# Windowed attention ahead of a SiLU MLP: attention in blocks with all heads, both key blocks side by side

## The chip, the cores and the metric

The kernel runs on one core of a Trainium2 chip. The metric is the device time of one execution in microseconds (us), the median of several runs. The engines are named as the profile names them: PE (TensorE, matrix products; PEld is its loading of weights), DVE (VectorE), ACT (ScalarE), POOL (GpSimd) and SP (SyncE, which issues most transfers).

## The reference

For 8 batches, 8 heads, 576 positions and head size 64 it computes attention in a causal window of 128 positions with a linear bias for each head, and sends the result (4608 tokens of 512 values) through an MLP with SiLU. Everything is float32; the MLP's weights are drawn as float64.

```python
scores = scale * np.matmul(q, k.transpose(0, 1, 3, 2))
mask = (rel >= 0) & (rel < window)
scores = np.where(mask, scores + bias[None], -1000000000.0)
attn = np.exp(scores - np.max(scores, axis=-1, keepdims=True))
attn = attn / (np.sum(attn, axis=-1, keepdims=True) + 1e-09)
x = np.matmul(attn, v)          # then to (tokens, 512)
h = x @ w_in                    # 512 x 2048
out = (h * (1.0 / (1.0 + np.exp(-h)))) @ w_out
```

## The kernel before, in words

**MLP.** Tokens go in nine groups of 512 (`TG`). For each group and each of 16 slices of the hidden size (`NF`) there are two half steps of the first product (`gemm1`, L464) and two of the second (`gemm2`, L499), of six products of 128x128 by 512 each. Every factor is split into a high and a low part of type float32r, and three of the four products of parts are made, so a group has 16 x 24 = 384 products. Between them stands the activation: tanh on ACT (`act1`, L471), a join on DVE (`act2`, L476), the high part on ACT (`act3`, L482), the low part `gl` (`act4`, L487) on POOL for the first 16 slices and on DVE for the others. In group 0 the weights are also converted: `w_next` loads float64 words, scales them on ACT (`w_split1`), joins three pieces on DVE (`w_shift` L533, `w_low` L538, `w_sign` L545), and takes the high part on ACT (L555) and the low part on POOL (L559); three of the 32 parts are converted ahead of the MLP.

**Attention.** Two batches follow each other in nine blocks of 128 rows (4 x 9 blocks in all). A unit is one block and two heads; there are 144 units and 16 ghosts, which only bring the keys and values of a block again. Inside a batch pair the order is heads first, blocks second (`plan`). A row of a block sees keys of its own block up to itself and of the block before behind itself, so exactly 128 keys; the kernel merges both blocks of scores into one tile of 128 columns: `soft1` (L277) copies the block before from PSUM on ACT, `soft_merge` (L286) lays the own block over it under a triangular mask on DVE. `row_max` (L292) adds the bias from `tab` and takes the row's maximum, `soft2` (L300) is the exponential on ACT. P is split into two float16 parts (`p_split`, L307 and L311), transposed by the DMA engines (L316), and parted again into its two key blocks by two selects on POOL (`p_select`, L355 and L358). `attend` (L382) multiplies with V, which is itself scaled by a power of two for each batch pair and split in two float16 parts (`v_hi` L222, `v_lo` L229). `normalize` divides by the sum and writes x, in two float16 parts from the ninth tile on.

The scores of the first 44 units (`QF`) come from float32 products of all 128 rows, with zeros in the other head's rows (L246). Later units split q and k in high and low parts (`qk_hi` on POOL L202 and L205, `q_lo` L210 and `k_lo` L215 on DVE) and make two float32r products of 256 columns for a head (L252). The first 16 units have P transposed by PE (L323) and V in float32.

**Order.** Each engine takes its instructions in the order in which the program writes them, and waits on semaphores that the framework sets. Ahead of the MLP `attn_cycle` runs 21 cycles of attention alone. From then on the points between half steps of the MLP are counted: `attn_item` puts a third of a cycle (scores; transposes; products with V) at a point, and `later(n, ...)` puts work of other engines n points later. PSUM has eight banks: tags `h` and `a` with two each, and `w`, `x`, `y`, `z`. During the MLP `w` to `z` hold the second product's sums, `h` the first's, and everything of attention shares `a`.

The scale of V needs a reduction over all V of a batch pair, nine reads and sums (`vscale_load`, `vscale_reduce`, `vscale_finish`).

## Time and profile before

| | |
|---|---|
| three runs | 1028.01 us median, 1027.22 to 1028.36 |
| span of the profiled execution, from its first to its last instruction | 1025.5 us; of its own time the profile gives no more than this |
| first product of the MLP | 52.7 us |
| first scaling of an output (group 0) | 211.5 us |
| busy: PE, DVE, ACT, POOL | 975.5, 748.8, 445.2, 450.6 us |
| mean granted clock of PE | 0.991 |
| transfers | 111.0 MB, of it HBM read 76.8 MB and written 9.4 MB |

Busy times are sums over the whole span; a share of it means little for a single stage, so the stages have to be looked at one by one. Products on PE are pipelined: the duration of one reaches into the next, and the pace is seen from the distances between starts. L12 is line 12 of the kernel.

### The profile page before, as it was taken

Reading aid. Unit: us, or ns where it says so; the run is one execution under the profiler, and the core shown is the slowest. Engines: PE = TensorE matmul, PEld = TensorE weight load, DVE = VectorE, ACT = ScalarE, POOL = GpSimd, SP = SyncE. Lnnn points to the kernel's source line nnn. Section 1 sums busy time; section 2 is a strip of 40 time slices with the busy share of each in tenths; the row PEclk is TensorE's granted clock in tenths of the full one; section 3 lists DMA queues with packets and bytes.
Section 4 is the critical chain, followed back from the end, with each engine's and each line's share of the span. In section 5 each row is a group of like instructions: output and inputs, shape, how many; then the busy total and the mean of one; then the engine's idle time right before and its main releaser. Section 6 shows DMA issues by size and latency. Waiting matters only on the chain.

```text
span 1025.5 us, 18152 instructions
## 1 busy us (share of the span) xinstructions
PE 975.5 (95%) x5832; PEld 798.2 (78%) x5832; DVE 748.8 (73%) x2306; ACT 445.2 (43%) x1039; POOL 450.6 (44%) x770
## 2 busy tenths in 40 slices
PE   7878777799999999999999999999999999999998
PEld 6866555678888888888888887888888888888886
DVE  4899999977777999777778997777699963223222
ACT  5755545444445444444444444343444442223222
POOL 2566576735344565543436665443465640001000
PEclk9999999899999999999999999999999999999999
DMA  8656565543345444543355445433453321011001
GB/s 288 198 145 193 178 176 162 157 113 104 83 106 131 119 109 122 131 115 88 91 115 130 121 116 140 96 81 74 119 119 98 98 81 27 1 21 42 1 1 41
DMA packets 166511, 111.04 MB, mean 108 GB/s; under 512 B 107920, under 2 KB 136592, under 8 KB 166416
## 3 DMA queue, kind: packets, MB, share of 16 engines
q1 hardware_dynamic: 165120, 107.53, 39.8%
q10 hardware_dynamic: 1296, 2.36, 0.7%
q8 instruction: 46, 0.75, 0.3%
q14 instruction: 49, 0.40, 0.1%
HBM read 76.81 MB, written 9.44 MB: 84 GB/s over the span
## 4 chain that ended last, share of the span: by engine, by line
PE 75%; DVE 16%; issue 4%; DMA 2%; ACT 2%; POOL 0%; SPq 0%; ACTq 0%; DVEq 0%; POOLq 0%
PE o L499 33%; PE h L464 32%; PE sp L252 4%; PE av L382 4%; DVE wm L538 3%; DVE v L229 2%; DVE wm L533 2%; DMA vm<-v 2%; DVE t L292 1%; DVE hr L311 1%; DVE t L286 1%; DVE wm L545 1%; PE sp L246 1%; DVE gt L476 1%; DMA rqk<-qk 1%
## 5 line engine op out<-in xcount | busy, mean ns | idle before, releaser
L464 PE MATMUL h<-xh,wih 128*128 128x512 f32 x576 | 231.7, 402 | 2.4 <-ACT wih L555 2.4
L499 PE MATMUL o<-woh,gh 128*128 128x512 f32 x576 | 231.6, 402 | 0.0
L464 PE MATMUL h<-xh,wil 128*128 128x512 f32 x576 | 227.5, 395 | 4.2 <-POOL wil L559 4.2
L499 PE MATMUL o<-woh,gl 128*128 128x512 f32 x576 | 227.8, 395 | 0.4 <-DVE gl L487 0.3
L499 PE MATMUL o<-wol,gh 128*128 128x512 f32 x576 | 226.9, 394 | 0.0
L464 PE MATMUL h<-xl,wih 128*128 128x512 f32 x576 | 226.4, 393 | 0.0
L476 DVE SCALAR_TENSOR_TENSOR gt<-gt,h 128x512 f32<-128x512 f32 x144 | 98.7, 685 | 141.8 <-ACT gt L471 141.2
L471 ACT ACTIVATE gt<-h 128x512 f32<-128x512 f32 x144 | 85.6, 594 | 199.3 <-PE h L464 197.8
L300 ACT ACTIVATE t<-t,mx 128x128 f32<-128x128 f32 x288 | 102.6, 397 | 146.7 <-DVE mx L292 143.2
L355 POOL TENSOR_SCALAR_AFFINE_SELECT po<-hl 128x512 f16<-128x512 f16 (+1 forms) x128 | 89.2, 697 | 116.5 <-DMA hl<-hr 98.8
L202 POOL TENSOR_SCALAR kh<-rqk 128x256 fp32r<-128x256 f32 x116 | 54.0, 465 | 182.4 <-PE sp L252 111.0
L464 PEld LDWEIGHTS h<-xh,wil 128*128 128x128 f32 x576 | 108.8, 189 | 31.5 <-POOL wil L559 7.6
L487 DVE TENSOR_TENSOR gl<-gt,gh 128x512 fp32r<-128x512 f32 x128 | 95.8, 749 | 49.5 <-ACT gh L482 48.6
L499 PEld LDWEIGHTS o<-woh,gl 128*128 128x128 f32 x576 | 108.3, 188 | 27.8 <-DVE gl L487 2.4
L464 PEld LDWEIGHTS h<-xh,wih 128*128 128x128 f32 x576 | 109.4, 190 | 23.5 <-ACT wih L555 3.5
L464 PEld LDWEIGHTS h<-xl,wih 128*128 128x128 f32 x576 | 109.3, 190 | 20.3 <-DVE xl L434 0.2
L499 PEld LDWEIGHTS o<-wol,gh 128*128 128x128 f32 x576 | 108.5, 188 | 20.4
L499 PEld LDWEIGHTS o<-woh,gh 128*128 128x128 f32 x576 | 108.4, 188 | 20.1
L482 ACT CAST gh<-gt 128x512 fp32r<-128x512 f32 x144 | 89.3, 620 | 52.9 <-DVE gt L476 50.6
L292 DVE CUSTOM_DVE_ANT_0 t<-t,tab 128x128 f32<-128x128 f32 x288 | 99.8, 383 | 4.8 <-DMA tab<-base 0.7
L358 POOL TENSOR_SCALAR_AFFINE_SELECT hl<-hl 128x512 f16<-128x512 f16 (+1 forms) x128 | 95.6, 747 | 8.8
L277 ACT COPY t<-sp 128x256 f32<-128x256 f32 (+2 forms) x128 | 45.3, 354 | 94.0 <-PE sp L252 79.6
(81 smaller groups left out, 1481.9 us busy)
## 6 DMA issues: line engine op xcount, KB each, us to landing
rqk<-qk SPq DMA_DIRECT2D x144, 256.0 KB, 2.8
rv<-v SPq DMA_DIRECT2D x144, 64.0 KB, 2.1
out<-ot SPq DMA_DIRECT2D x36, 256.0 KB, 2.0
wr<-w_in SPq DMA_DIRECT2D x16, 512.0 KB, 3.9
wr<-w_out SPq DMA_DIRECT2D x16, 512.0 KB, 3.5
vm<-v SPq DMA_DIRECT2D x27, 256.0 KB, 3.0
vm<-v ACTq DMA_DIRECT2D x9, 256.0 KB, 5.0
rqk<-qk SPq DMA_DIRECT2D x16, 128.0 KB, 2.2
```

The costliest lines, as they stand in the source:

```text
L202: nc.gpsimd.tensor_scalar(kh[:, s], rqk[:, 1], 1.0, 1.0, op0=ALU.mult, op1=ALU.mult)
L277: nc.scalar.copy(t[rows, :, cols], sp[rows, :, o, cols])
L292: nc.vector.tensor_tensor_reduce(out=t[:, h], in0=t[:, h], in1=tab[:, 2 * hp + h], scale=-0.125, scalar=3.0e38, op0=ALU.add, op1=ALU.min, ...
L300: nc.scalar.activation(t[:, h], t[:, h], AF.Exp, bias=mx[:, h : h + 1], scale=-1.0)
L355: nc.gpsimd.affine_select(out=po, in_=hl, pattern=dims + [[-1, P]], base=-1, channel_multiplier=1, compare_op=ALU.is_ge, fill=0.0)
L358: nc.gpsimd.affine_select(out=hl, in_=hl, pattern=dims + [[1, P]], base=0, channel_multiplier=-1, compare_op=ALU.is_ge, fill=0.0)
L464: nc.tensor.matmul(hps[n], w[:, cc], x, start=(half == 0 and i == 0), stop=(half == 1 and i == len(seq) - 1), skip_group_check=True,)
L471: nc.scalar.activation(gt, hps[n], AF.Tanh, scale=0.5 / W_SCALE)
L476: nc.vector.scalar_tensor_tensor(out=gt, in0=gt, scalar=1.0, in1=hps[n], op0=ALU.add, op1=ALU.mult)
L482: nc.scalar.copy(gh, gt)
L487: (nc.gpsimd if GLP(n) else nc.vector).tensor_sub(gl, gt, f32(gh))
L499: nc.tensor.matmul(ops[ti], a[:, t], w, start=(f == 0 and i == 0), stop=(f == NF - 1 and i == len(seq) - 1), skip_group_check=True,)
```

## The change

Attention is written anew. The unit of work is now a pair: one block and four heads (`p`, two to a block, 72 in all). Blocks come in order, each with all heads, so there are no ghosts; keys and queries of a block are loaded once for all heads (256 KB each, against 256 KB for each unit before).

- **Scores** are float32 products for every block. The tile has the 64 rows of one head in its upper half and those of the next in its lower half; each product takes 64 rows, and neighbouring products are of different halves and go to different PSUM banks. The splitting of q and k is gone.
- **Both key blocks lie side by side** in tiles of 256 columns. `tab` holds the bias for 256 columns with -1e30 where the window ends, so the copy, the merge and the two selects are gone; the maxima read PSUM directly, and the exponentials, both parts of P and its transposes are twice as wide. Where two batches meet, DVE writes the mask into PSUM (`other_batch`).
- **P** is always transposed by the DMA engines, and V always in two float16 parts, a whole block of 512 columns at a time.
- **x** of the first four tiles is float32 and is transposed by PE; later ones are multiplied to float32 and split on ACT and DVE (`x_hi`, `x_lo`).
- **Engines**: `gl` is made on POOL in all groups; the low parts of `w_in` are made on DVE, those of `w_out` still on POOL. Four weight parts are converted ahead of the MLP.
- **Order**: one list of points. Pair p has its scores at point 8(p - 8) - 26 and its other work at fixed distances from there; points below 0 lie ahead of the MLP, and a group of the MLP has 64 points. During the MLP the scores of a pair take both buffers of tag `a`, which products with V and the scales of V use too.

```diff
-NPAIR = H // 2
+NHP = H // 2
...
+NPAIR = 2 * NTILE
...
-KSLOTS = 4
-VSLOTS = 5
+KSLOTS = 3
+VSLOTS = 3
...
+STEP = 8
+LEAD = 26
+XD = GT
...
+WD = (1, 1, 1, 2, 3)
+W_EARLY = (-52, -40, -28, -14)
...
+def at(p):
+    return STEP * (p - 2 * GT) - LEAD
...
-    tab = const.tile([P, H, P], BF16, name="tab")
+    tab = const.tile([P, H, 2 * P], BF16, name="tab")
...
-    bank = {"scores": ["a"], "pt": ["a"], "av": ["a"], "misc": ["a"]}
+    bank = {"scores": [("w", "x"), ("y", "z")], "av": ["a"], "misc": ["h"]}
...
-        tag = (LAST[-1], LAST[-2], "vraw")[i % 3 if b == 0 else 2]
+        tag, bufs = (LAST[4 + i % 4], 1) if b == 0 else ("rv", 2)
...
-    def qk_hi(u):
...
-    def q_lo(u):
...
-    def k_lo(u):
...
-    def soft0(u):
...
-    def soft1(u):
...
-    def soft_merge(u):
...
-    def p_select(u):
...
+    def load_k(i):
+        ks[i] = pool.tile([P, NHP, P], F32, tag="k", bufs=KSLOTS, name=f"k{i}")
+        nc.sync.dma_start(ks[i], qk[i, 1])
+    def load_q(i):
+        qs[i] = pool.tile([P, NHP, P], F32, tag="q", bufs=2, name=f"q{i}")
+        nc.sync.dma_start(qs[i], qk[i, 0])
+    def v_hi(i):
+        rv = rvs[i].rearrange("p (h d) -> p h d", h=H)
+        nc.gpsimd.tensor_scalar(
+            v1[:, i % VSLOTS, :, 0:D], rv, vsc[i // NBLK][:, 0:1], 1.0, op0=ALU.mult, op1=ALU.mult
+        )
+    def v_lo(i):
+        rv = rvs.pop(i).rearrange("p (h d) -> p h d", h=H)
+        nc.vector.scalar_tensor_tensor(
+            out=v2[:, i % VSLOTS], in0=rv, scalar=vsc[i // NBLK][:, 0:1], in1=v1[:, i % VSLOTS, :, 0:D],
+            op0=ALU.mult, op1=ALU.subtract,
+        )
+    def scores(p):
+        i, q = divmod(p, 2)
+        tags = next_tag("scores")
+        sp = [ps_of(tags[h], f"sp{p}_{h}").rearrange("p (u o c) -> p u o c", u=2, o=2) for h in range(2)]
+        for u in range(2):
+            for o in range(blocks(p).start, 2):
+                for h in range(2):
+                    rows = slice(h * D, (h + 1) * D)
+                    nc.tensor.matmul(
+                        sp[h][:, u, o], qs[i][rows, 2 * q + u], ks[i - 1 + o][rows, 2 * q + u],
+                        start=True, stop=True, skip_group_check=True,
+                    )
+        st[p] = {"sp": sp, "t": {}, "hl": {}, "mx": pool.tile([P, 4], F32, tag="mx", bufs=4, name=f"mx{p}")}
+    def other_batch(p):
+        for h in range(2):
+            cols = st[p]["sp"][h].rearrange("p u o c -> p u (o c)")
+            if block_of(p // 2) == SPLIT:
+                nc.vector.memset(cols[HALF:, :, : P + HALF], MASKED)
+            elif block_of(p // 2) == SPLIT + 1:
+                nc.vector.memset(cols[:, :, :HALF], MASKED)
+    def row_max(p, u):
+        q, o = p % 2, blocks(p)
+        n = (o.stop - o.start) * P
+        st[p]["t"][u] = t = pool.tile([P, 2, 2 * P], F32, tag="t", bufs=3, name=f"t{p}_{u}")
+        for h in range(2):
+            nc.vector.tensor_tensor_reduce(
+                out=t[:, h, 2 * P - n :], in0=st[p]["sp"][h][:, u, o].rearrange("p o c -> p (o c)"),
+                in1=tab[:, 4 * q + 2 * u + h, 2 * P - n :], scale=-0.125, scalar=3.0e38,
+                op0=ALU.add, op1=ALU.min, accum_out=st[p]["mx"][:, 2 * u + h : 2 * u + h + 1],
+            )
+    def exps(p, u):
+        t, n = st[p]["t"][u], (2 - blocks(p).start) * P
+        for h in range(2):
+            x = t[:, h, 2 * P - n :]
+            nc.scalar.activation(x, x, AF.Exp, bias=st[p]["mx"][:, 2 * u + h : 2 * u + h + 1], scale=-1.0)
+    def split_of(p, u, what):
+        n = 2 - blocks(p).start
+        return what[:, : 4 * n * P].rearrange("p (a h c) -> p a h c", a=2, h=2)
+    def p_hi(p, u):
+        t, n = st[p]["t"][u], (2 - blocks(p).start) * P
+        st[p]["hr", u] = hr = pool.tile([P, 8 * P], F16, tag="hr", bufs=2, name=f"hr{p}_{u}")
+        nc.scalar.activation(split_of(p, u, hr)[:, 0], t[:, :, 2 * P - n :], AF.Copy, scale=PSCALE)
+    def p_lo(p, u):
+        t, n = st[p]["t"][u], (2 - blocks(p).start) * P
+        hr = split_of(p, u, st[p]["hr", u])
+        nc.vector.scalar_tensor_tensor(
+            out=hr[:, 1], in0=t[:, :, 2 * P - n :], scalar=PSCALE, in1=hr[:, 0], op0=ALU.mult, op1=ALU.subtract
+        )
+    def p_transpose(p, u):
+        n = 2 - blocks(p).start
+        hr = st[p].pop(("hr", u))
+        st[p]["hl"][u] = hl = pool.tile([P, 8, P], F16, tag="hl", bufs=4, name=f"hl{p}_{u}")
+        nc.sync.dma_start_transpose(hl[:, : 4 * n], hr[:, : 4 * n * P])
...
+    def normalize(p, stage):
+        (i, q), av = divmod(p, 2), st[p]["av"]
+        if stage == 0:
+            st[p]["r"] = r = pool.tile([P, 4, 1], F32, tag="r", bufs=3, name=f"r{p}")
+            total = av[:, :, D : D + 1]
+            if i < XD:
+                nc.vector.tensor_scalar(r, total, PSCALE * EPS, vsc[i // NBLK][:, 0:1], op0=ALU.add, op1=ALU.mult)
+            else:
+                nc.vector.tensor_scalar_add(r, total, PSCALE * EPS)
+            nc.vector.reciprocal(r, r)
+            return
+        if i < XD:
+            if i not in xt:
+                xt[i] = pool.tile([P, DM], F32, tag=LAST[i], bufs=1, name=f"x{i}")
+            x = xt[i][:, q * 4 * D : (q + 1) * 4 * D]
+        else:
+            st[p]["x"] = x = pool.tile([P, 4 * D], F32, tag="xs", bufs=2, name=f"xs{p}")
+        nc.vector.tensor_mul(
+            x.rearrange("p (h d) -> p h d", h=4), av[:, :, 0:D], st[p]["r"].to_broadcast([P, 4, D])
+        )
+    def x_hi(p):
+        i, q = divmod(p, 2)
+        if i < XD:
+            return
+        if q == 0:
+            xt[i] = pool.tile([P, 2, DM], F16, tag="x", bufs=4, name=f"x{i}")
+        nc.scalar.copy(xt[i][:, 0, q * 4 * D : (q + 1) * 4 * D], st[p]["x"])
+    def x_lo(p):
+        i, q = divmod(p, 2)
+        if i >= XD:
+            cols = slice(q * 4 * D, (q + 1) * 4 * D)
+            nc.vector.tensor_sub(xt[i][:, 1, cols], st[p]["x"], xt[i][:, 0, cols])
+            if q == 1:
+                whole.append(i)
+        del st[p]
...
-        (nc.gpsimd if GLP(n) else nc.vector).tensor_sub(gl, gt, f32(gh))
+        nc.gpsimd.tensor_sub(gl, gt, f32(gh))
...
-        nc.gpsimd.tensor_sub(lo, wraw.pop((f, which))[1], f32(hi))
+        (nc.gpsimd if which else nc.vector).tensor_sub(lo, wraw.pop((f, which))[1], f32(hi))
...
+    for p in range(NPAIR):
+        i, q = divmod(p, 2)
+        n = at(p)
+        put(n, scores, p)
+        if block_of(i) in (SPLIT, SPLIT + 1):
+            put(n + 1, other_batch, p)
+        put(n + 1, row_max, p, 0)
+        put(n + 2, row_max, p, 1)
+        put(n + 2, exps, p, 0)
+        put(n + 3, exps, p, 1)
+        put(n + 3, p_hi, p, 0)
+        put(n + 4, p_lo, p, 0)
+        put(n + 4, p_hi, p, 1)
+        put(n + 4, p_transpose, p, 0)
+        put(n + 5, p_lo, p, 1)
+        put(n + 5, p_transpose, p, 1)
+        put(n + 20, attend, p)
+        put(n + 21, normalize, p, 0)
+        put(n + 22, normalize, p, 1)
+        put(n + 23, x_hi, p)
+        put(n + 24, x_lo, p)
+        if q == 0:
+            if i > 1:
+                put(n - 14, load_q, i)
+                put(n - 14, load_k, i)
+            put(n - 2, load_v, i)
+            put(n + 9, v_hi, i)
+            put(n + 10, v_lo, i)
+    for b in range(1, NBB):
+        n = at(2 * NBLK * b)
+        for i in range(VCH):
+            put(n - 10 * STEP + i * STEP, vscale_load, b, i)
+            put(n - 10 * STEP + i * STEP + 6, vscale_reduce, b, i)
+        for x in range(3):
+            put(n - 6 + 2 * x, vscale_finish, b, x)
...
+        while pos[0] < 0:
+            begin()
+            pos[0] += 1
+        bank.update(scores=[("a", "a")], misc=["a"])
...
+                        later(1, act2, n)
+                        later(2, act3, n)
+                        later(2, act4, n)
...
+                if g == 0 and half == 0:
+                    w_next()
```

More of the change, by code (lines that the diff above doesn't have):

```diff
@@ L279, in soft_merge @@
-    def soft_merge(u):
-        b, hp, j, _ = units[u]
-        sp, d, o = st[u]["sp"]
-        t = st[u]["t"]
-        for a in (slice(0, HALF), slice(HALF, P)) if j == SPLIT else (slice(0, P),):
-            n = a.stop - a.start
-            mask = tri.bitcast(I32)[a, :, a].to_broadcast([n, 2, n])
-            nc.vector.copy_predicated(t[a, :, a], mask, sp[a, :, d, a])
-    def row_max(u):
-        b, hp, j, _ = units[u]
-        t, mx = st[u]["t"], st[u]["mx"]
-        for h in range(2):
-            nc.vector.tensor_tensor_reduce(
-                out=t[:, h], in0=t[:, h], in1=tab[:, 2 * hp + h], scale=-0.125, scalar=3.0e38,
-                op0=ALU.add, op1=ALU.min, accum_out=mx[:, h : h + 1],
-            )
@@ L387, in normalize @@
[L387 to L399 removed]
+    xt, whole, now = {}, [], [0]
@@ L442, in x_send @@
     def x_send():
-        for i in [i for i in whole if i * P // TG <= now[0] + 1]:
+        if not w_done():
+            return
+        for i in [i for i in whole if i // GT <= now[0] + 1]:
             whole.remove(i)
@@ L593, in w_next @@
             w_split1(*a)
[L594 removed]
+            for fn, n in zip((w_shift, w_low, w_sign, w_hi, w_last), WD):
                 later(n, fn, *a)
             later(WD[2], w_next_load)
[L598 to L616 removed]
```

564 lines of the change are left out of this document (104 added, 460 removed).

## The prediction

> **What bounds the kernel now.** I read the page's span first, then the span cut at the borders of the MLP's groups, then the work inside each stretch. The columns of the cut are the stretch, its length, the busy time of PE, PEld, DVE, ACT and POOL, the granted clock, the share of the DMA engines and GB/s. The borders are the first product of the MLP (52.7 us) and the first ScalarE scaling of a group's output (211.54 us for group 0), behind which half of its last products (1.4 us) are still to come; 842, 932 and 1020.5 us are found in the same way.
>
> ```profile
> span 1025.5 us, 18152 instructions
> ...
> 0.00:52.70 52.70, 41.87 (x308) 39.17 (x308) 35.29 (x171) 33.64 (x99) 22.02 (x66) 0.94 0.74 237
> 52.70:213.00 160.30, 128.96 (x799) 99.85 (x797) 152.03 (x326) 85.72 (x193) 107.05 (x115) 0.97 0.57 162
> 213.00:842.00 629.00, 625.99 (x3915) 513.95 (x3914) 509.60 (x1719) 281.05 (x674) 317.54 (x584) 1.00 0.44 108
> 842.00:932.00 90.00, 90.00 (x433) 73.13 (x433) 27.73 (x57) 23.50 (x39) 4.00 (x6) 1.00 0.10 25
> 932.00:1020.50 88.50, 88.50 (x386) 72.09 (x384) 23.47 (x34) 21.16 (x35) 0.00 (x0) 1.00 0.04 13
> ...
> L464 PE MATMUL h<-xh,wih x576: 387/392/695, 52.7 to 1014.3; 128*128 128x512 f32 x192
> ...
> 211.54 0.60 ACT L509 ACTIVATE ot<-o 128x512 f32<-128x512 f32 x1
> ```
>
> There are three regimes. Ahead of 52.7 us only attention runs. In group 0 (160.3 us) DVE is busy 152.0 us: it is the bound. From 213 us PE has no gap. The last group has no attention and takes 88.5 us for its 384 products, 0.230 us each; groups 1 to 6 take 629.0 us, 98 us above six times 88.5, and group 7 1.5 us above it. PE is thus the bound there, and attention's products are paid in full: 99.5 us. What remains behind 1020.5 us (5.0 us) are the last scaling and stores, which the change leaves alone.
>
> **The products of attention.** These rows give paces by the distances of their starts; the durations overlap.
>
> ```profile
> 8.28 0.39 PE L246 MATMUL sp<-rqk 128*128 128x128 f32 x2
> 8.50 0.39 PE L246 MATMUL sp<-rqk,rqk 128*128 128x128 f32 x2
> 12.36 0.39 PE L382 MATMUL av<-vf,hl 128*128 128x65 f32 x2
> 12.58 0.39 PE L382 MATMUL av<-vf,po 128*128 128x65 f32 x2
> 23.45 0.63 PE L246 MATMUL sp<-rqk,rqk 128*128 128x128 f32 x2
> 23.88 0.64 PE L246 MATMUL sp<-rqk 128*128 128x128 f32 x2
> ...
> 401.67 0.26 PE L382 MATMUL av<-v,po 128*128 128x65 f16 x3
> 402.04 0.48 PE L464 MATMUL h<-xh,wih 128*128 128x512 f32 x1
> 402.36 0.40 PE L464 MATMUL h<-xl,wih 128*128 128x512 f32 x1
> ...
> L252 PEld LDWEIGHTS sp<-kl,qhl 128*128 128x128 f32 x208 | 39.3, 189 | 5.6 <-DVE kl L215 1.3
> ```
>
> A float32 product is two instructions: 128 columns take 0.22 us (8.28 to 8.50), 0.43 us at the low clock (23.45 to 23.88), and 65 columns as long (12.36 to 12.58), so it is as much the loading of the weights as the columns. Twelve float16 products with P take 0.37 us, 0.031 us each (401.67 to 402.04, four rows of three). The split scores have 208 products with kl, two to a unit: 104 units, all of groups 1 to 6, and 98 / 104 = 0.94 us a unit. A pair of the new kernel (four heads of a block) replaces two units: 1.88 us before.
>
> Its 24 float16 products stay: 0.74 us. Its scores are 8 float32 products, 16 instructions of 0.111 us, on 64 rows each. If neighbours in different halves run together, 16 instructions need about 17/2 steps: 0.94 us; if not, 1.78 us. No row of before has two products in different halves. I take the lower end, since two such products share neither rows nor a PSUM bank, and keep 1.78 us as a rival. Turns: behind attention the second MLP product starts 0.32 instead of 0.23 us after the first (402.04 to 402.36), 0.09 us lost, for each of a pair's two visits. The change between whole array and halves has no row; I give it one more turn, 0.10 us, between nothing and the 0.16 us by which the end of a product (0.39 us) lies behind the start of the next. A pair: 0.94 + 0.74 + 0.18 + 0.10 = 1.96 us, between 1.68 (no turns) and 2.86.
>
> On this the Trainium skill, TensorEngine Tiling (Array Packing), section Tiling Modes, speaks both ways: tiles of the array may load weights and multiply in parallel, and a change of the tiling drains the engine. By the first a pair's scores cost the lower end; by the second it pays two drains, which at 0.16 us each instead of the 0.10 would make 52 x 0.22 = 11 us more. No run here shows either for halves.
>
> Positions: a pair's scores stand at 8(p-8)-26, so pairs 0 to 11 come ahead of the MLP, 12 to 19 in group 0 and 20 to 71 in groups 1 to 7, four of them with one key block. That is 50 x 0.94 + 53 x 0.74 + 52 x 0.19 + 55 x 0.09 = 101 us against 99.5. The V scales now share their PSUM tag with scores and attention: three times a wait for a normalization, 0.5 us, and its way, 2 us in all (0 to 6). With 1.6 us for the next item **groups 1 to 8 cost +5 us** (-10 to +50 by the ends for a pair).
>
> **gl on GpSimd.** `act4` goes from DVE to POOL in every group.
>
> ```profile
> L487 DVE TENSOR_TENSOR gl<-gt,gh 128x512 fp32r<-128x512 f32 x128 | 95.8, 749 | 49.5 <-ACT gh L482 48.6
> L487 POOL TENSOR_TENSOR gl<-gt,gh 128x512 fp32r<-128x512 f32 x16 | 22.5, 1407 | 7.1 <-ACT gh L482 6.8
> ```
>
> 1.41 us instead of the 0.69 of an undisturbed one on DVE (307.27, below). PE is the cover: `gl` of a step is asked for after four half steps of 1.38 us. In the step with a pair ACT, at prices from the first stage below, does `act1` (0.5), four exps (0.41 each), one `p_hi` (0.52) and only then `act3` (0.5). Counted from the end of the scores: `act1` begins at 2.8, `gh` is there at 6.2 and with the ways between engines at 6.6, `gl` at 8.1, and PE asks for it at 2.8 + 2.8 + 0.8 (attention) + 2.8 + 0.5 = 9.7. Free, with 1.5 us in hand. At the end of a group only two steps lie between; scores at position 62 cover the lack, but not in groups 7 and 8: 1.0 + 0.6 us.
>
> **Group 0.** Weights are converted here, and DVE is the bound.
>
> ```profile
> L538 DVE SCALAR_TENSOR_TENSOR wm<-wr,wm 128x512 int32<-128x512 int32 x29 | 30.3, 1044 | 1.0
> ...
> 100.60 1.31 POOL L559 TENSOR_TENSOR wol<-wm,woh 128x512 fp32r<-128x512 f32 x1 [0.24 <-ACT woh L555]
> ...
> 100.69 1.36 DVE L229 SCALAR_TENSOR_TENSOR v<-rv,vsc,v 128x128 f16<-128x128 f32 x1
> ...
> 112.53 0.42 DVE L533 TENSOR_SCALAR wm<-wm 128x512 int32<-128x512 int32 x1
> 112.98 1.00 DVE L538 SCALAR_TENSOR_TENSOR wm<-wr,wm 128x512 int32<-128x512 int32 x1
> 118.62 0.69 DVE L538 SCALAR_TENSOR_TENSOR wm<-wr,wm 128x512 int32<-128x512 int32 x1
> 119.35 0.69 DVE L545 SCALAR_TENSOR_TENSOR wm<-wr,wm 128x512 int32<-128x512 int32 x1
> 119.96 0.43 DVE L286 COPY_PREDICATED t<-tri,sp 128x256 f32<-128x256 int32 x1
> 120.43 0.29 DVE L292 CUSTOM_DVE_ANT_0 t<-t,tab 128x128 f32<-128x128 f32 x1
> 120.65 0.29 DVE L292 CUSTOM_DVE_ANT_0 t<-t,tab 128x128 f32<-128x128 f32 x1
> ...
> 307.27 0.69 DVE L487 TENSOR_TENSOR gl<-gt,gh 128x512 fp32r<-128x512 f32 x1
> 307.87 0.42 DVE L311 SCALAR_TENSOR_TENSOR hr<-t,hr 128x256 f16<-128x256 f32 x1
> ```
>
> Undisturbed starts are 0.73 us (118.62 to 119.35) and 0.61 us apart for the two joins, 0.45 us for the shift (112.53 to 112.98), 0.22 us for a 128-column row maximum with its read-out (120.43 to 120.65), 0.60 us for 512 columns (307.27 to 307.87): 1.0 ns a column between, so 0.34 us for 256. The first join averages 1044 ns here. The `v` row says why: 128 columns should take about 0.3 us, like the row maximum, and it ends only when POOL's `wol`, begun 0.09 us earlier, has ended. At such paces DVE's work in group 0 before is 29 weight parts x 1.79 = 52, 16 `act2` x 0.60 = 10, and 19 units of about 2 us, 39: 101 us. The row of the stretch says 152, so 51 us are stretch behind POOL's 107 us, and 8 idle.
>
> After, per pair: four row maxima of 256 columns 1.4 us; two `p_lo` of 512 1.2; half a `v_lo` of 512 0.3; normalizing (256 columns and two short ones) 0.5; `x_lo` of 256 0.34: 3.7 us, 30 us for eight pairs. 28 weight parts x 1.79 = 50; 14 low parts moved from POOL to DVE x 0.60 = 8; `act2` 16 x 0.60 = 10; `xl`, stores, scale 4. Sum 103 us. POOL loses all selects: 16 gl x 1.41 + 14 low parts x 1.31 + five V parts of about 1 us (four times the columns of `v` before) = 46 us. Stretch by POOL's time: 51 x 46/107 = 22 to 24; idle 8 as before. **135 us** against 160.3. Ends: no stretch and no idle 105 (PE's own 88.5 + 8 x 1.96 = 104), full stretch 162.
>
> **Ahead of the MLP.** Twelve pairs instead of 21 units, both key blocks wide.
>
> ```profile
> 30.76 0.70 ACT L300 ACTIVATE t<-t,mx 128x128 f32<-128x128 f32 x2
> 31.36 0.36 ACT L331 COPY hl<-pt 128x256 f32<-128x256 f32 x1
> 31.61 0.64 ACT L143 ACTIVATE vm<-vm 128x512 f32<-128x512 f32 x1
> ...
> 7.49 5.02 DMA vm<-v
> 13.29 7.15 DMA vm<-v
> ...
> L316 SPq DMA_TRANSPOSE hl<-hr x124: 1188/1190/2697, 64.8 to 863.3; - x124
> ...
> xt<-x SPq DMA_TRANSPOSE x28, 3.1
> ```
>
> Nine reads of V again gate its scale, until 13.29 + 7.15 = 20.4 us; pair 1 waits behind that on DVE. Then a cycle: maxima begin, four exps follow at 0.41 us each (30.76 to 31.36 is two of 128 columns, 0.30 each, and 128 columns more cost half of the 0.25 us from 31.36 to 31.61, less what is fixed in it: 0.11), then two `p_hi` of 512 columns at 0.52; begun 0.45 us behind the first maximum they end at 3.1, the second `p_lo` at 3.8, normalizing at 4.3 us. Order lets neither engine run ahead, so ten pairs take 43 us. Four weight parts add 8, the other batch's memsets and the first x 4: **75 us** against 52.7 (68 where weights hide in gaps, 85 if PE at the low clock paces: 8 x 0.43 + 1.5 = 4.9 us a pair).
>
> The transposes double in size, not in number per head pair: SP holds 1.19 us for 512 columns, and 1024 land in 3.1 us as `xt` shows. Fifteen positions lie between them and attention, so they are hidden everywhere; with two waits for `hr` and `hl` still in hand they'd be late in the first stage only, by under 3 us.
>
> **Sum.** 75 + 135 = 210 against 213: -3. With +5: 1025.5 - 3 + 5 = 1027.5 us of the profiled execution, which lies 2.5 under the median of the runs: **1030 us**, own range 1016 to 1046. The gain of group 0 (25 us) is eaten ahead of it (22 us).
>
> **Rivals.** *Halves don't run together* (the change doesn't do what it says): 0.84 x 50 = 42 us in groups 1 to 7 and 0.5 x 10 ahead: 1077. For: 65 columns cost what 128 do, so weights set the pace, and nothing shows two loads together. Against: the interleaving of heads and banks makes no conflict. It decides from any overlap under half.
>
> *The stretch goes.* Group 0 near 111 us: 1006. For: the new row maximum reads PSUM, and the `gt` join, which does too, averages 681 ns in group 0, like the undisturbed 512 columns at 307.27. Against: 73 of the 103 us (weights 58, `p_lo` 10, `v_lo` and `x_lo` 5) still take two inputs from SBUF or stand between such, and POOL still has 30 long subtractions. It decides if they fall into DVE's PSUM work. The Trainium skill, SBUF — State Buffer, section Who interferes with whom, has it as a rule: two SBUF inputs on VectorE contend with a GpSimd read, one doesn't, and the later is blocked whole; the trace agrees (the `v` row, 1.36 us).
>
> ```profile
> L476 DVE SCALAR_TENSOR_TENSOR gt<-gt,h 128x512 f32<-128x512 f32 x16 | 10.9, 681 | 1.2 <-ACT gt L471 1.1
> ```
>
> *gl comes late.* If DVE or ACT lag 1.4 us more in the steps with a pair, PE waits: 0.5 us in each of 52, 1056. Against: at the prices above DVE has 40 and ACT some 40 of a group's 104 us.
>
> **How the numbers follow.** Forecast 0.45, halves apart 0.27, stretch gone 0.20, gl late 0.08. 0.2% (2 us) is what a measurement tells from no change. The forecast's own spread gives 0.13 under 1026, 0.10 within, 0.22 above; so faster 0.33, same 0.10, slower 0.57. The range 1007 to 1079 leaves out the lower half of the third and a third of the second.
>
> **What would show it.** First MLP product near 75 us and the end of group 0 near 210; DVE 85% or more in between; starts of neighbouring scores under 0.06 us apart on average against 0.11; 13 us a pair in groups 1 to 6 and 88 to 90 us in group 8. PE waits on `gl` over 10 us, or a first stage outside 68 to 85, make it wrong.

## The result, and the profile after

The changed kernel takes **1053.44 us** (median of four runs, 1053.21 to 1053.94), beside 1027.62 (1025.47 to 1028.36) for the kernel before on the same chip: a ratio of 1.0255 with a 95% interval of 1.0239 to 1.0271, so 26 us slower. Predicted were 1030 us, with a range of 1007 to 1079.

First the span cut at the same borders as before (columns: stretch, its length, busy time of PE, PEld, DVE, ACT and POOL, granted clock, share of the DMA engines, GB/s), then the row of the MLP's first product, from a view of that line, and the first scaling of group 0's output.

```profile
span 1052.2 us, 16631 instructions
...
0.00:20.00 20.00, 3.54 (x21) 2.77 (x23) 2.98 (x18) 9.34 (x25) 0.95 (x8) 1.00 0.81 254
20.00:86.80 66.80, 34.55 (x363) 29.28 (x362) 48.00 (x161) 36.07 (x77) 6.70 (x8) 0.69 0.83 188
86.80:220.50 133.70, 111.49 (x697) 86.35 (x695) 122.00 (x237) 80.53 (x163) 48.20 (x38) 0.99 0.65 174
220.50:859.00 638.50, 628.92 (x4130) 503.68 (x4129) 301.61 (x846) 279.74 (x600) 155.39 (x145) 1.00 0.43 95
859.00:960.00 101.00, 99.12 (x618) 79.92 (x617) 37.53 (x97) 37.85 (x75) 24.54 (x22) 1.00 0.26 58
960.00:1047.80 87.80, 87.18 (x384) 71.55 (x383) 12.39 (x18) 20.82 (x35) 20.55 (x16) 1.00 0.03 10
...
L344 PE MATMUL h<-xh,wih x576: 387/389/775, 86.9 to 1041.4; 128*128 128x512 f32 x192
...
219.09 0.60 ACT L390 ACTIVATE ot<-o 128x512 f32<-128x512 f32 x1 [1.32 <-PE o L379]
```

| stretch | before | predicted | after | after less before |
|---|---|---|---|---|
| ahead of the MLP | 52.7 | 75 | 86.8 | +34.1 |
| group 0 | 160.3 | 135 | 133.7 | -26.6 |
| groups 1 to 8 | 807.5 | 812.5 | 827.3 | +19.8 |
| end | 5.0 | 5.0 | 4.4 | -0.6 |

The four sum to the 26.7 us between the spans. Group 0 came out within 1.3 us of the prediction; ahead of the MLP and in groups 1 to 8 the kernel lost 12 and 15 us more than predicted. In both of them no engine explains its stretch by its work alone: ahead of the MLP (second row) DVE is busy 48.0 of 66.8 us and PE 34.6, and in groups 1 to 6 (fourth row) PE leaves 9.6 us idle, where before it left 3.0. Of the 19.8 us of groups 1 to 8, 10.7 are more busy time of PE and 9.1 more idle time.

What PE waits for in groups 1 to 8 (waits, total, times, longest):

```profile
PE av L261 <- DVE mx L214: 6.2, 7, 2.1
PE o L379 <- POOL gl L367: 5.7, 12, 0.7
```

And the products of attention of two pairs in the middle of group 3, by starts:

```profile
465.96 0.39 PE L379 MATMUL o<-woh,gl 128*128 128x512 f32 x1
466.19 0.90 PE L261 MATMUL av<-v,hl 128*128 128x65 f16 x24
466.92 0.48 PE L344 MATMUL h<-xh,wih 128*128 128x512 f32 x1
467.23 0.39 PE L344 MATMUL h<-xl,wih 128*128 128x512 f32 x1
...
472.24 0.39 PE L379 MATMUL o<-woh,gl 128*128 128x512 f32 x1
472.56 1.16 PE L194 MATMUL sp<-k,q 64*128 64x128 f32 x16
473.65 0.50 PE L344 MATMUL h<-xh,wih 128*128 128x512 f32 x1
473.99 0.39 PE L344 MATMUL h<-xl,wih 128*128 128x512 f32 x1
```

The 16 score instructions take 1.09 us (472.56 to 473.65), entering them costs 0.32 instead of 0.23 us, leaving them 0.34 instead of 0.23; the 24 products with V take 0.73 and leaving them 0.31. A pair so takes 1.09 + 0.09 + 0.11 + 0.73 + 0.08 = 2.10 us, where 1.96 were predicted and two units took 1.88 before.

### The profile page after: what moved, and what is told of

Read it like the earlier page. It is cut to its first block, busy times and chain, and to the rows that moved or that the text cites. A ratio compares the mean times of both kernels' runs of the same rounds, so it can differ in the third digit from the quotient of the medians.

```text
span 1052.2 us, 16631 instructions
## 1 busy us (share of the span) xinstructions
PE 965.3 (92%) x6204; PEld 773.6 (74%) x6204; DVE 525.2 (50%) x1374; ACT 464.8 (44%) x975; POOL 256.3 (24%) x236
## 5 line engine op out<-in xcount | busy, mean ns | idle before, releaser
L367 POOL TENSOR_TENSOR gl<-gt,gh 128x512 fp32r<-128x512 f32 x144 | 187.7, 1303 | 637.5 <-ACT gh L362 428.6
L344 PE MATMUL h<-xh,wih 128*128 128x512 f32 x576 | 237.6, 413 | 0.0
L379 PE MATMUL o<-woh,gh 128*128 128x512 f32 x576 | 225.4, 391 | 0.2 <-ACT gh L362 0.2
L379 PE MATMUL o<-wol,gh 128*128 128x512 f32 x576 | 224.3, 389 | 0.0
L238 DVE SCALAR_TENSOR_TENSOR hr<-t,hr 128x512 f16<-128x512 f32 (+1 forms) x144 | 131.3, 912 | 91.8 <-ACT hr L233 91.1
L214 DVE CUSTOM_DVE_ANT_0 t<-sp,tab 128x256 f32<-128x256 f32 (+1 forms) x288 | 103.2, 403 | 80.3 <-PE sp L194 80.3
L224 ACT ACTIVATE t<-t,mx 128x256 f32<-128x256 f32 (+1 forms) x288 | 121.2, 487 | 27.3 <-DVE mx L214 26.5
L194 PE MATMUL sp<-k,q 64*128 64x128 f32 x1088 | 93.0, 309 | 23.0 <-DMA k<-qk 6.5
L194 PEld LDWEIGHTS sp<-k,q 64*128 64x128 f32 x1088 | 76.9, 207 | 46.8 <-issue 44.9
L261 PEld LDWEIGHTS <-hl 128*128 128x128 f16 x1632 | 57.5, 101 | 51.6 <-issue 36.9
```

The source lines that it names most:

```text
L194: nc.tensor.matmul(sp[h][:, u, o], qs[i][rows, 2 * q + u], ks[i - 1 + o][rows, 2 * q + u], start=True, stop=True, skip_group_check=True,)
L214: nc.vector.tensor_tensor_reduce(out=t[:, h, 2 * P - n :], in0=st[p]["sp"][h][:, u, o].rearrange("p o c -> p (o c)"), in1=tab[:, 4 * q + 2 ...
L224: nc.scalar.activation(x, x, AF.Exp, bias=st[p]["mx"][:, 2 * u + h : 2 * u + h + 1], scale=-1.0)
L238: nc.vector.scalar_tensor_tensor(out=hr[:, 1], in0=t[:, :, 2 * P - n :], scalar=PSCALE, in1=hr[:, 0], op0=ALU.mult, op1=ALU.subtract)
L261: nc.tensor.matmul(av[:, 2 * u + h, : rhs.shape[-1]], lhs, rhs, start=(n == 0), stop=(n == len(seq) - 1), skip_group_check=True,)
L344: nc.tensor.matmul(hps[n], w[:, cc], x, start=(half == 0 and i == 0), stop=(half == 1 and i == len(seq) - 1), skip_group_check=True,)
```

## The experiments

Each kernel is the changed kernel with one edit unless it says otherwise. The table gives, in us, the first product of the MLP, the way from there to the first scaling of group 0's output, from that to the same scaling of the last group, the median, and the ratio to the kernel before. Stretches that an edit does not touch differ by up to 1.4 us in the first column, 0.6 in group 0 and 3.7 in groups 1 to 8. Nearly all of these 3.7 us lie in group 1, from 105.4 (e_pet) to 108.9 us (e_vlate) between the scalings; groups 2 to 8 together differ by no more than 0.5. What group 1 hangs on is told in the last section. The kernel before took 1027.0 to 1028.2 us beside these runs.

| run | first product | group 0 | groups 1 to 8 | median | ratio, 95% |
|---|---|---|---|---|---|
| before | 52.7 | 158.8 | 807.1 | 1027.6 | 1 |
| after | 86.9 | 132.2 | 827.2 | 1053.4 | 1.0239 to 1.0271 |
| e_heads_apart | 85.8 | 132.3 | 851.3 | 1079.1 | 1.0473 to 1.0521 |
| e_gl_dve | 85.5 | 132.4 | 818.5 | 1046.6 | 1.0160 to 1.0209 |
| e_rm | 84.8 | 136.1 | 816.8 | 1045.6 | 1.0153 to 1.0192 |
| e_wide | 88.2 | 132.4 | 823.8 | 1051.7 | 1.0213 to 1.0252 |
| e_g0nogl | 86.1 | 122.9 | 826.0 | 1043.4 | 1.0135 to 1.0175 |
| e_chain | 83.3 | 132.4 | 826.3 | 1050.5 | 1.0199 to 1.0242 |
| e_vlate | 87.6 | 132.4 | 828.0 | 1055.0 | 1.0243 to 1.0285 |
| e_first | 80.1 | 132.7 | 827.7 | 1047.6 | 1.0174 to 1.0213 |
| e_half | 83.4 | 132.3 | 827.2 | 1049.9 | 1.0190 to 1.0248 |
| e_pet | 74.7 | 132.1 | 824.3 | 1038.6 | 1.0088 to 1.0129 |
| e_pbest | 76.8 | 135.7 | 808.5 | 1028.6 | 0.9997 to 1.0026 |
| e_pbest2 | 73.5 | 133.2 | 809.9 | 1023.5 | 0.9933 to 0.9970 |

### Do the halves run together? (e_heads_apart)

```diff
-        for u in range(2):
-            for o in range(blocks(p).start, 2):
-                for h in range(2):
+        for h in range(2):
+            for u in range(2):
+                for o in range(blocks(p).start, 2):
```

> Scores of a pair in the order head, u, key block, so that neighbouring products are of the same half of the array; nothing else differs. Theory (neighbours in different halves run together, which is why 16 instructions take 1.09 us instead of 16 x 0.111 = 1.78): 0.69 us more for each of 50 full pairs in groups 1 to 7, 35 us; 1053 becomes about 1088. Rival 1 (64 rows alone make an instruction shorter): no change, 1053. Rival 2 (PE at the low clock paces the first stage): 2.08 us a pair there becomes about 3.4, so some 13 us more ahead of the MLP as well, about 1100.

Measured: 25.6 us slower than the changed kernel, less than the 35 expected, and nearly all of it in groups 1 to 8 (+24.1). Scores of a pair there:

```profile
312.78 1.71 PE L193 MATMUL sp<-k,q 64*128 64x128 f32 x16
314.42 0.50 PE L343 MATMUL h<-xh,wih 128*128 128x512 f32 x1
```

1.64 us instead of 1.09: 0.55 us more, 26 us for the 48 full pairs of these groups. So the halves do overlap when neighbours alternate. Strict alternation isn't needed, though: the four pairs with one key block have four instructions of one half and then four of the other in this kernel, and these take 0.66 us (453.14 to 453.80), where the changed kernel takes 0.64. Only the runs of eight cost more; why was not tried. The first product of the MLP does not come later (85.8 against 86.9 us): ahead of the MLP the scores' pace is not what counts, and rival 2 falls.

### Loads or columns? (e_wide)

All keys stay in one tile, and where the two blocks are neighbours in it one product of 256 columns takes the place of two.

```diff
-        ks[i] = pool.tile([P, NHP, P], F32, tag="k", bufs=KSLOTS, name=f"k{i}")
+        ks[i] = kall[:, i % KSLOTS]
...
+            if blocks(p).start == 0 and i % KSLOTS:
+                for h in range(2):
+                    rows = slice(h * D, (h + 1) * D)
+                    nc.tensor.matmul(
+                        sp[h][:, u], qs[i][rows, 2 * q + u], kall[rows, (i - 1) % KSLOTS : i % KSLOTS + 1, 2 * q + u],
+                        start=True, stop=True, skip_group_check=True,
+                    )
+                continue
```

> All keys lie in one buffer, and in the blocks where both key blocks are neighbours in it (two of three) one product of 256 columns takes the place of two of 128: half the weight loads for the same columns. Theory, that the loading of weights paces the scores (0.11 us a 128-column instruction, of which the columns alone are the lesser part): the 16 instructions of 1.09 us become 8 that take 0.8 to 0.9 us, 0.2 to 0.3 us a pair in 33 of 50 pairs, so 6 to 10 us faster. Rival, that the columns pace: 8 instructions take the 1.09 us that 16 took, and the time stays within 1.5 us.

Measured: 1.7 us faster; of the 3.4 us in groups 1 to 8, 2.9 lie in group 1 and only 0.4 in the others. The row of a pair, and beside it, from the changed kernel, a pair of a block with one key block only:

```profile
471.11 1.13 PE L194 MATMUL sp<-kall,q 64*128 64x256 f32 x8
472.18 0.50 PE L352 MATMUL h<-xh,wih 128*128 128x512 f32 x1
```

```profile
447.36 0.71 PE L194 MATMUL sp<-k,q 64*128 64x128 f32 x8
448.00 0.50 PE L344 MATMUL h<-xh,wih 128*128 128x512 f32 x1
```

Half the loads take 1.07 us for the columns that took 1.09: the columns pace, and the theory of e_wide falls. Half the columns with half the loads take 0.64 us, so eight instructions more cost 0.45 us, 0.056 each: two halves that run together completely, and 0.19 us fixed for a visit.

### gl on GpSimd (e_gl_dve, e_g0nogl)

```diff
-        nc.gpsimd.tensor_sub(gl, gt, f32(gh))
+        (nc.gpsimd if n < NF else nc.vector).tensor_sub(gl, gt, f32(gh))
```

> gl on VectorE from group 1 on, as before the change. Theory (5.7 us of waits of PE on gl behind the groups' borders are the price of GpSimd, VectorE has room): 5 to 6 us less, about 1047.5. Rival (VectorE's row maxima and low parts come later for it, and attention's products wait instead): between 1051 and 1056.

Measured: 6.9 us faster, groups 1 to 8 shorter by 8.7 (6.3 in groups 2 to 8, 2.3 in group 1), and no wait of PE on `gl` is left in them. The waits of 5.7 us were real and not hidden.

In group 0 the question was the other one, whether POOL's reads stretch DVE's work:

```diff
+        if n < NF:
+            nc.gpsimd.memset(f32(gl), 0.0)
+            return
         nc.gpsimd.tensor_sub(gl, gt, f32(gh))
```

> In group 0 alone the low part gl is set to zero by a memset on GpSimd (which reads nothing) instead of computed from gt and gh: the low part of the hidden values is left out for the first 512 tokens. Theory (DVE's work in group 0 is stretched by GpSimd's reads in proportion to GpSimd's time, 22 us of stretch by 48 us): DVE's busy time in group 0 falls from 122 by 8 to 11 us, and group 0 from 133.7 by as much. Rival (the rest of the stretch goes with the weight parts and the V parts, or DVE's busy time is its own work): DVE's busy time and the group fall by under 3 us.

Group 0 of this kernel in the cut by stretches:

```profile
86.10:210.40 124.30, 110.68 (x695) 87.12 (x694) 112.45 (x237) 80.50 (x163) 31.00 (x37) 0.97 0.67 188
```

DVE has the same 237 instructions and is busy 112.5 instead of 122.0 us; the group is 9.4 us shorter (124.3 against 133.7). The theory holds: DVE's work is longer by 9.6 us with POOL's subtractions beside it, and group 0 gets shorter as DVE does. What POOL's other work costs DVE in group 0 was not tested.

### The row maxima at the start of a group (e_rm)

In the trace of after, DVE's second scaling of group 0's output waits 3.35 us for a buffer that a store still holds, and the second pair of row maxima stands behind it:

```profile
223.44 0.39 PE L344 MATMUL h<-xh,wil 128*128 128x512 f32 x1
224.30 0.69 DVE L388 TENSOR_SCALAR ot<-o 128x512 f32<-128x512 f32 x1 [3.35 <-DMA out<-ot]
224.91 0.74 DVE L176 SCALAR_TENSOR_TENSOR v<-rv,vsc,v 128x512 f16<-128x512 f32 x1
225.57 0.28 DVE L214 CUSTOM_DVE_ANT_0 t<-sp,tab 128x128 f32<-128x128 f32 x1
225.92 0.91 PE L261 MATMUL av<-v,hl 128*128 128x65 f16 x24 [2.08 <-DVE mx L214]
226.64 0.78 PE L344 MATMUL h<-xh,wih 128*128 128x512 f32 x1
227.21 0.63 PE L344 MATMUL h<-xl,wih 128*128 128x512 f32 x1
```

Products with V need one of the two PSUM buffers that the scores hold until their maxima are read.

```diff
-        put(n + 2, row_max, p, 1)
+        put(n + 1, row_max, p, 1)
```

> The second two row maxima of a pair are issued one point earlier, so that at the start of a group DVE does them before its scaling of the old group's output, for which it must wait for PE's last product. Theory: the 6.2 us in seven waits of attention's products on the row maxima go (in the changed kernel the products of the pair before stand behind scores that wait for this PSUM room), at most 2 us are left of them, the kernel is 4 to 6 us faster than the changed kernel and nothing else moves. Rival: the wait only changes its name (scores' room, or the store scaling now late), gain under 1.5 us.

Measured: 7.8 us faster, more than expected; groups 1 to 8 are 10.4 us shorter (6.4 in groups 2 to 8, 3.8 in group 1), the wait is gone and PE's waits on `gl` fall from 5.7 to 4.0 us. But group 0 is 3.9 us longer, where PE now waits for `gh` (6.2 us) and `gl` (5.8) in place of the maxima (12.6 before the edit). The expectation that nothing else moves was wrong: in group 0 DVE is busy nine tenths of the time, and what is put ahead there pushes the MLP's own items back. That this is the whole cause is not shown: the granted clock in group 0 was lower too, 0.92 instead of 0.99. A lower clock alone did not lengthen the group in e_chain, where 0.94 went with 132.4 us.

### Ahead of the MLP (e_chain, e_vlate, e_first, e_half, e_pet)

The cycle that was predicted at 4.3 us, from a pair's first maximum to the next pair's, in the trace of after:

```profile
23.50 0.42 DVE L214 CUSTOM_DVE_ANT_0 t<-sp,tab 128x256 f32<-128x256 f32 x1
23.96 1.70 ACT L224 ACTIVATE t<-t,mx 128x256 f32<-128x256 f32 x4 [0.87 <-DVE mx L214]
25.76 0.63 ACT L233 ACTIVATE hr<-t 128x512 f16<-128x512 f32 x1
26.43 0.69 DVE L238 SCALAR_TENSOR_TENSOR hr<-t,hr 128x512 f16<-128x512 f32 x1 [1.47 <-ACT hr L233]
27.11 0.51 PE L261 MATMUL av<-v,hl 128*128 128x65 f16 x6 [0.88 <-DMA hl<-hr]
27.15 0.63 ACT L233 ACTIVATE hr<-t 128x512 f16<-128x512 f32 x1 [0.75 <-DMA hl<-hr]
27.45 3.25 SPq L246 DMA_TRANSPOSE hl<-hr  x2
27.81 0.69 DVE L238 SCALAR_TENSOR_TENSOR hr<-t,hr 128x512 f16<-128x512 f32 x1 [0.34 <-ACT hr L233]
28.42 0.42 DVE L285 TENSOR_TENSOR x<-av,r 128x256 f32<-128x256 f32 x1
28.75 0.41 DVE L214 CUSTOM_DVE_ANT_0 t<-sp,tab 128x256 f32<-128x256 f32 x1
```

5.25 us. The chain is the predicted one up to 26.4; then ACT waits 0.75 us until a transpose has left its `hr` buffer, and the rest comes that much later. In SP's own queue the four transposes from 27.45 on take 8.69 us; at the median of 1.23 us for one, 4.9 of that are their own and the rest is waiting:

```profile
27.45 8.69 SPq L246 DMA_TRANSPOSE hl<-hr  x4
36.19 0.57 SPq L166 DMA_DIRECT2D rv<-v  x1
```

From pair 2 (23.50) to pair 11 (84.70) nine cycles take 61.2 us, 6.8 each with the weights. Five edits asked what holds them.

**e_chain** takes DVE's wait for ACT out of the pair: for pairs 0 to 9 `p_lo` and the transposes come seven points later, with more buffers for `t` and `hr`.

```diff
-        put(n + 4, p_lo, p, 0)
+        late = 7 if p < 10 else 0
+        put(n + 4 + late, p_lo, p, 0)
         put(n + 4, p_hi, p, 1)
-        put(n + 4, p_transpose, p, 0)
+        put(n + 4 + late, p_transpose, p, 0)
...
```

> For pairs 0 to 9 the low part of P and its transpose come 7 points later, behind the row maxima of the next pair, with room for P and its parts taken from the MLP's tiles that are still empty. Theory (ahead of the MLP the order on VectorE and ScalarE makes each wait for the other, and the high part of P waits for the transposes' buffers): a pair goes from 5.9 us to about 4.4, 12 to 15 us less ahead of the MLP, group 0 unchanged, about 1040. Rival (PE at the low clock or the transfers pace the first stage): under 3 us less, above 1050.

**e_vlate** spreads the V sums behind pair 1 and puts the scale of V ahead of pair 2 instead of pair 1.

```diff
-            put(n + 9, v_hi, i)
-            put(n + 10, v_lo, i)
+            put(n + (9 if i else 18), v_hi, i)
+            put(n + (10 if i else 19), v_lo, i)
...
-            put(at(0) + 1 + i // 2, vscale_reduce, 0, i)
+            put(at(0) + 2 + 3 * i // 2, vscale_reduce, 0, i)
...
-            put(at(0) + 6 + x, vscale_finish, 0, x)
+            put(at(0) + 15 + x, vscale_finish, 0, x)
```

> The sums and the scale of V of the first batches are made later (points +2 to +17 instead of +1 to +8), so pair 1 isn't queued behind them on VectorE and PE. Theory (VectorE idles from 8.5 to 19.9 us only because of that order): pair 1's maxima start near 15 us, 4 to 5 us less in all, about 1048.5. Rival (the scale is needed by the first products with V anyway, and the wait only moves there): 1052 to 1055.

Measured: 2.9 us faster and 1.5 slower, in both cases the time that the rival gave. In e_chain PE now waits 22.1 us in all for the transposes' landing ahead of the MLP, and scores of the next pairs stand behind those products in PE's order. One row of its cut speaks against PE's clock as the pace (first e_chain, then the changed kernel, same borders):

```profile
24.90:80.10 55.20, 32.90 (x344) 28.07 (x344) 42.99 (x139) 32.30 (x69) 6.00 (x7) 0.91 0.86 203
```

```profile
24.90:80.10 55.20, 29.32 (x316) 24.65 (x316) 40.07 (x131) 30.84 (x64) 5.32 (x6) 0.69 0.85 186
```

At a granted clock of 0.91 instead of 0.69 the stage was only 3.6 us shorter.

**e_first** gives everything behind `p_lo` the same seven points (pairs 0 to 7) and more buffers for `hl`, spreads the V sums, and transposes x earlier.

```diff
-        put(n + 20, attend, p)
+        put(n + 20 + late, attend, p)
...
+        for cc, n in enumerate((-8, -7, -3)):
+            put(n, x_transpose, cc)
```

> Ahead of the MLP: p_lo, the transposes and everything behind them of pairs 0 to 7 come seven points (about one pair) later, with as many more buffers for t, hr and hl; the V sums and the V scale are spread behind pairs 1 and 2 instead of in front of pair 1; and the transposes of x come as soon as their pairs are there instead of behind pair 11. Theory (the cycle of about 5.7 us a pair is a chain through DVE, ACT, DVE and the landing of the transposes, no engine's own work): DVE's own 3.7 us and PE's 4.3 to 4.9 us a pair at the low clock now pace, ten pairs take 45 to 52 instead of 61 us, and the first MLP product comes at 68 to 76 instead of 86.8: 11 to 18 us faster. Rival (the SP queue and the landing of the transposes, or PE at the low clock, pace already): the waits change names as when only p_lo was moved, first product at 82 or later, gain under 5 us.

Measured: first product at 80.1, 5.9 us faster: between the two expectations, so it decides nothing. SP's queue of this kernel shows why more room did not help more:

```profile
19.89 13.34 SPq L246 DMA_TRANSPOSE hl<-hr  x3
33.33 0.53 SPq L166 DMA_DIRECT2D rv<-v  x1
33.95 0.39 SPq L161 DMA_DIRECT2D q<-qk  x1
34.39 0.42 SPq L157 DMA_DIRECT2D k<-qk  x1
```

SP stood 13 us at three transposes, most of it because their `hr` was not ready, and the reads of v, q and k behind them waited too.

**e_half** asks whether the transfers themselves pace: transposes of half the columns, as many of them.

```diff
-        nc.sync.dma_start_transpose(hl[:, : 4 * n], hr[:, : 4 * n * P])
+        m = 2 * n if p < 12 else 4 * n
+        nc.sync.dma_start_transpose(hl[:, :m], hr[:, : m * P])
```

> The DMA transposes of pairs 0 to 11 carry only the high half of P, 512 columns instead of 1024; SP holds each as long as before. The products with the low part take the high part again (as many products, but the low part of P is left out ahead of the MLP). Theory now (20.0 to 86.8 us have the 16 DMA engines busy for 83%, 55 us; 25 plain transfers of 7.2 MB at the 398 GB/s of the stretch from 4 to 8 us are some 18 us of that, so 20 transposes have 37 us, 1.8 each, 3.7 a pair, and the transfers, not the engines' own work, pace the cycle of 5.5 to 6 us): the DMA engines' busy time falls by some 18 us and the first MLP product comes 8 to 15 us earlier, at 72 to 79. Rival (the chain of DVE, ACT and PE, or SP's hold of 1.23 us a transpose, paces; the landing is 1 to 2 us shorter, seen only where attention waits): 0 to 4 us earlier.

```profile
20.00:86.80 66.80, 38.13 (x375) 32.98 (x375) 49.80 (x168) 37.34 (x81) 7.69 (x8) 0.72 0.58 148
```

The share of the DMA engines falls from 0.83 to 0.58, 16.7 us of busy time, and the first product comes 3.5 us earlier (83.4). The rival holds: not the transfers' bandwidth.

**e_pet** takes these pairs off SP and the DMA engines altogether: PE transposes P, and ACT and DVE split it on its way out of PSUM, one pair later in the order and with more buffers for `t`.

```diff
+        for h in range(2):
+            for o in range(n):
+                nc.tensor.transpose(pt[:, a : a + P], t[:, h, c : c + P], ident)
...
+        if p < 10:
+            for u in range(2):
+                put(n + 9 + u, pe_transpose, p, u)
+                put(n + 9 + u, pe_hi, p, u)
+                put(n + 11 + u, pe_lo, p, u)
```

> For pairs 0 to 9 P is transposed on PE in float32, as the kernel before did for its first units (four transposes of 128 columns for two heads, into the PSUM banks that lie idle ahead of the MLP), and split into high and low part on its way out of PSUM, by the same two instructions of ACT and DVE as before, one pair later in the order: nothing of these pairs goes through SP or a DMA transpose, and DVE never waits for ACT inside a pair. Theory (transposes by DMA and the order behind them pace the first stage): PE gets 8 x 0.22 us more a pair, DVE's 3.7 us and PE's 4 to 5 us pace, ten pairs take 45 to 50 instead of 61 us, first MLP product at 71 to 77, 10 to 16 us faster than the changed kernel. Rival (PE at a granted clock near 0.7 becomes the bound with 2.1 + 1.6 + 3.4 us a pair): 7 us a pair, no gain or up to 10 us slower.

```profile
20.00:74.00 54.00, 35.98 (x443) 31.43 (x444) 48.81 (x169) 35.12 (x79) 7.21 (x8) 0.88 0.42 133
...
L366 PE MATMUL h<-xh,wih x576: 387/389/776, 74.7 to 1026.3; 128*128 128x512 f32 x192
```

First product at 74.7, 12.2 us earlier, and the kernel 14.8 us faster. DVE is busy 48.8 of 54.0 us, 90%, with as much work as before: it is nearly full now. So 12 of the 34 us ahead of the MLP are the way of P through `hr`, SP and the landing, and the order around it; which of the waits on that way holds at each moment was not separated. Nor was the granted clock of PE, 0.88 here instead of 0.69; e_chain and e_heads_apart speak against it as the cause.

### Together (e_pbest, e_pbest2)

e_pbest is e_pet, e_vlate's V sums, x transposed early (at -19, -18 and -5), e_gl_dve, e_rm and e_wide.

> The same with the V sums spread behind pair 1, the transposes of x as soon as their pairs are there, gl on DVE from group 1 on, the row maxima one point earlier and the 256-column products. If the gains add up: 12 to 16 us ahead of the MLP, 7 of gl, 5 to 8 of the row maxima, 1.7 of the wide products, 26 to 33 us under the changed kernel, 1020 to 1027: at or just under the kernel before. If the first stage does not gain: 1037 to 1040.

Measured: 1028.6 us, no difference from the kernel before. Against e_pet its first product is 2.1 us later and group 0 3.6 us longer. e_rm had lost as much in group 0; ahead of the MLP PE waits 8.0 us for DVE's `hl` at the early transposes of x.

e_pbest2 leaves these two out, moves the maxima from pair 20 on only, and takes two weight parts apart while DVE is idle:

```diff
-W_EARLY = (-52, -40, -28, -14)
+W_EARLY = (-86, -86, -46, -28, -14)
...
+        put(n + (1 if p >= 20 else 2), row_max, p, 1)
```

> What the runs so far single out, together: transposes on PE for pairs 0 to 9, gl on DVE from group 1 on, the row maxima one point earlier from pair 20 on only (in group 0 they made the group 3.8 us longer), the 256-column products, V sums and transposes of x as in the changed kernel, and two weight parts taken apart in the idle time of DVE between 9 and 19 us (five ahead of the MLP instead of four). Summed from the runs: first product at 74.7 less up to 2.4 for the weights moved out of the busy stretch, group 0 133.5 less 2.4 for one part fewer, groups 1 to 8 808.5, end 4.4: 1016 to 1021 of the profiled execution and 1018 to 1023 of the median, 0.4 to 0.9% under the kernel before. Rival (the weight parts delay the V scale by their 1.3 us of ACT, or the row maxima's gain hung on their place in group 0): 1025 to 1030, no difference from before.

Measured: **1023.47 us** (1021.82 to 1025.43), 0.48% under the kernel before (0.30 to 0.67%), 0.5 us above what was expected: the first product came only 1.2 us earlier than in e_pet, and group 0, with one weight part less, took 133.2 instead of 132.1 us. The scale of V comes 2.2 us later than in e_pet (23.9 instead of 21.7), behind the two weight parts on DVE, as the rival feared; that this held the first product back is likely but not shown.

```profile
23.87 0.14 DVE L147 COPY vsc<-vs 128x2 f32<-128x2 f32 x1
...
L374 PE MATMUL h<-xh,wih x576: 387/389/795, 73.5 to 1012.3; 128*128 128x512 f32 x192
```

## Why the prediction was right, and where it was wrong

The range held the result, and most of the chance (0.57) lay on the side of slower; the likeliest case was 23 us too low. That the range held is in part luck: its upper end, 1079 us, came from the rival with halves apart, which did not happen. The forecast's own range, 1016 to 1046, missed by 7 us, and of the 0.57 only 0.22 were for a slower kernel by the forecast's own mechanism.

- **Group 0, right.** 135 predicted, 133.7 measured. DVE's 103 us and 22 to 24 of stretch are 122.0 in the trace, with 11.7 us idle where 8 were assumed: two misses of 3 to 5 us that cancel. That about half of the stretch comes from POOL's subtractions is shown by e_g0nogl: these (16 of 1.47 us in the changed kernel, 23.5) cost DVE 9.6 us, 0.41 us for each us, not far from the 51/107 that the prediction scaled by. The Trainium skill, SBUF — State Buffer, section Who interferes with whom, says this of two SBUF inputs on VectorE beside a GpSimd read; the run agrees (122.0 against 112.5 us of DVE). The rival *the stretch goes* fell with it.
- **The halves, right in the mechanism, a little too cheap.** 0.94 us for a pair's scores was 1.09: 16 steps of 0.056 us, as reckoned, and 0.19 us fixed (e_wide). The sign that the prediction asked for, under 0.06 us between starts on average, was missed through the fixed part (1.09/16 = 0.068). The Trainium skill, TensorEngine Tiling (Array Packing), section Tiling Modes, lets tiles of the array work in parallel (the trace agrees, 1.09 against 1.64 us) and drains at a change. The turns of a pair's scores cost 0.09 us in and 0.11 out, 0.20 where the prediction had 0.19 (0.09 for a turn and 0.10 for the change) and feared two drains of 0.16. Leaving the products with V, where the tiling stays, costs 0.08, so no more than a few hundredths can be the drain's. The rival *halves don't run together* was priced too high: 47 us above the forecast, where e_heads_apart is 25.6 above the changed kernel, since a pair's scores took 1.64 us and not 1.78 and the first stage did not grow. That e_heads_apart's 1079 us lie beside the rival's 1077 is luck, because the changed kernel itself stands 23 us above the forecast.
- **Ahead of the MLP, wrong: 75 predicted, 86.8 measured,** outside the 68 to 85 that the prediction had set for itself. The step that failed is "they are hidden everywhere ... they'd be late in the first stage only, by under 3 us". The transposes and the order behind them cost 12 us (e_pet). The 4.3 us were worked out as if only ACT and DVE were in the ring; `hr` has two buffers, which a transpose must leave first, SP takes nothing else meanwhile, and the reads of q, k and v for later pairs stand behind it (8.69 us for four transposes from 27.45). The low clock on PE, which the upper end of 85 was made of (ten pairs at its 4.9 us make 81 by its own sum), is not the pace as far as e_chain and e_heads_apart show.
- **Groups 1 to 8, the term was mis-sized: +5 predicted, +19.8 measured.** A pair cost 2.10 instead of 1.96 us, some 7 us over 50 pairs. `gl` was reckoned as free with 1.5 us in hand in the step with a pair, and as 1.6 us at borders; it cost 5.7 us of waits, and taking them away gave 6.3 us in groups 2 to 8. The third part was not in the sum at all: at the start of a group DVE stands at the scaling of the old output while the maxima of a new pair, which hold both PSUM buffers, wait behind it; PE's waits for it were 6.2 us, and another order gave 10.4 (e_rm), 1.4 of them from the slow stretch of the last section. The prediction named the shared PSUM tag, but priced it for the V scales alone. Measured singly, `gl` and the maxima give 6.3 and 6.4 us in groups 2 to 8, and with the wide products' 0.4 they give 13.2 together (e_pbest2), so there the parts add up. In group 1 they give 2.3 and 3.8 singly and 4.0 together: the slow stretch of the last section is missing in the traces of both, and it can be saved only once.
- **The rival *gl comes late*** would have been 26 us, 0.5 us in each of 52 steps; in groups 1 to 8 it came 12 times, 0.3 to 0.7 us each, at the ends and starts of groups, not in the steps with a pair. Its limit of 10 us of waits wasn't reached.

## What to carry to other kernels

A ring of work that leaves an engine and comes back through a transfer has to be reckoned with its buffers and with everything that stands behind it in the issuing queue: two engines' durations gave 4.3 us where the ring took 5.3 to 6, although no engine, and not the DMA's bandwidth either, was full. Look for the borders of stages: waits of 0.3 to 2 us that come two or three times a group were 12 of the 20 us lost in groups 1 to 8, and half of them lay in the order of instructions on an engine that was busy half its time. When a fused order loses against the old one, its parts may still be good; here a new route for P and a few moves of order and engine turned 2.5% slower into 0.5% faster.
